# A two-layer MLP in a spectral kernel: the first layer's 512-column products become pairs of 256, and its operands change their byte places

## The chip, the core and the metric

The kernel runs on one core of a Trainium2 chip. Its engines are TensorE (PE, with the weight loads shown as PEld), VectorE (DVE), ScalarE (ACT), GpSimd (POOL) and SyncE (SP), which issues most of the DMAs. The metric is the time of one execution on the device in microseconds. Three runs of the kernel before gave 1358.87, 1359.84 and 1359.89 us, a median of 1359.84.

## The reference

Everything is float32, for 4 sequences of 3136 tokens with 256 features.

```
X = rfft(x, axis=1);  y = irfft(X * (filt_r + 1j*filt_i), n=3136)      # a filter along the sequence
mixed = real(fft(fft(y, axis=1), axis=2));  u = y + mixed               # a Fourier mix
un = layer_norm(u);            v = u + relu(un @ w_ch1) @ w_ch2         # first MLP  (256 -> 1024 -> 256)
vn = layer_norm(v) * g_ln;     out = v + relu(vn @ w_ch1') @ w_ch2'     # second MLP (256 -> 1024 -> 256)
```

## The kernel before

The Fourier transforms of length 3136 = 64 x 49 are written as small matrix products. They run partly ahead of the two MLPs (sequence 0, about the first 100 us) and partly between their products (sequences 1 to 3). The MLPs take the largest part of the time, and the change touches only their first layer.

The tokens are cut into 25 units: units 0 to 23 have 512 tokens (four tiles of 128), unit 24 has 256. A block is one unit in one of the two MLPs, and it has eight steps, one for each 128 of the 1024 hidden features. `steps` lists 400 steps, 384 of them with 512 tokens. In the main loop step i issues the first layer of step i + 2 (`w1_step`, L906), then whatever small work is due at that place (transforms, normalization, the input of later units), then the second layer of step i (`w2_step`, L934), then the evictions of the first layer of step i + 2 (`w1_evict`, L916 on ScalarE and L917 on VectorE). This order is written out by hand; each engine runs its own instructions in it.

To come near float32 accuracy each operand is split in a high and a low part in the type fp32r, and a product a*b becomes high*high + low*high + high*low. So the first layer has six products for a step (two halves of the 256 features, three terms), all of them accumulated in one PSUM bank of 512 columns. The stationary operand (`lhsT`) is a 128 x 128 piece of the weights `w1a` or `w1b`, the moving one (`rhs`) the transposed input `xth` or `xtl` with one column per token. The second layer is the other way round: stationary is a 128 x 128 piece of the first layer's output (`hh` or `hl`, one piece for each tile of 128 tokens), moving a 128 x 256 piece of the weights `w2a` or `w2b`. A step has twelve such products, and they write the four halves of two banks in turn. Every matmul instruction becomes a weight load (LDWEIGHTS) and a product (MATMUL) on the chip.

The other products that stand between the MLP steps are L731 (256 columns, the Fourier mix), L267 (quarter products of 64 x 64 or less for the transforms), and the transposes L618 and L831 (128 columns).

Where a tile lies in SBUF is set by the order of the pools and by `PAD`, seven gaps in 4-byte words, of which `gap2` stands ahead of the first-layer weights, `gap3` ahead of the second-layer weights, `gap5` ahead of the transposed inputs and `gap6` ahead of the h buffers. In bytes modulo 256 the kernel before has its operands at these places:

| operand | tiles | place |
|---|---|---|
| first layer, stationary | w1a, w1b | 32 |
| first layer, moving | xth, xtl | 96 |
| second layer, stationary | hh, hl | 0 |
| second layer, moving | w2a, w2b | 192 |
| L731, stationary | zsh, zsl | 64 |
| L731, moving | chi, clo | 0 |

All slices that these products take begin at multiples of 512 bytes from the tile's start, so each product has its tile's place.

Of the kernel before, what the change touches and what calls it, by code (L numbers as in the profile page):

```python
# [34 lines left out]
CS, o = {}, 0  # L35
# [123 lines left out]
    return c.astype(np.float32)  # L159


PAD = (24, 16, 56, 40, 16, 8, 40)
NA, LAG = 3, 3
AHEAD = 3
DURING = {4: 'a', 8: 'a', 12: 'a', 16: 'a', 18: 'k', 20: 'a', 24: 'ac', 26: 'a', 28: 's', 30: 'f', 31: 'c', 33: 'f', 34: 'c', 35: 'f', 37: 'f', 38: 'c'}
# [18 lines left out]
def spectral_mlp_kernel(ctx: ExitStack, tc, x, ff, ff0, cst, w1a, w2a, gln, w1b, w2b, out):  # L184
    nc = tc.nc
# [3 lines left out]
    def pool(name, bufs, **kw):  # L189
        return ctx.enter_context(tc.tile_pool(name=name, bufs=bufs, **kw))  # L190

    def gap(name, words):
        pool(name, 1).tile([128, words], F32, name=name)

    sm = pool("sm", 4)
    head = pool("head", 1)
    gap("gap0", PAD[0])
    keep = pool("keep", 1)
    gap("gap1", PAD[1])
    keep64 = pool("keep64", 1)  # L200
    uop = pool("uop", 1)
    gap("gap2", PAD[2])
    wp1 = pool("wp1", 1)
    gap("gap3", PAD[3])
    wp2 = pool("wp2", 1)
    wps = {"1": wp1, "2": wp2}
    dram = pool("dram", B, space=DRAM)
    ztp = pool("ztp", 2)
    gap("gap4", PAD[4])
    zsp = pool("zsp", 1)  # L210
# [10 lines left out]
    xdp = pool("xdp", 2, space=DRAM)  # L221
    gap("gap5", PAD[5])
    xtp = pool("xtp", 2)
# [4 lines left out]
    def bank(k=1):  # L228
        t = banks.tile([128, 512], F32, tag="b", name="ps")
        return t if k == 1 else t.rearrange("p (a d) -> p a d", a=k)  # L230
# [9 lines left out]
    def weight(n):  # L240
        if n not in wt:
            wt[n] = wps[n[0]].tile([128, 2, 2, H] if n[0] == "1" else [128, 2, 8, D], F32R, tag="w" + n, name="w" + n)
        return wt[n]
# [417 lines left out]
    def tiles(U):  # L661
        return 4 if U < NU else 2
# [233 lines left out]
    def w1_step(U, layer, m):  # L896
        n = tiles(U) * 128
        assert all(("1" + "ab"[layer], j) in conv_done for j in range(4)), (U, layer, m)
        w = weight("1" + "ab"[layer])
        xt = xt_of[U, layer]  # L900
        ps = bank()
        i = 0
        o = ps[:, :n]
        for k in range(2):
            for a, s in ((0, "h"), (1, "h"), (0, "l")):
                nc.tensor.matmul(out=o, lhsT=w[:, a, k, m * 128:m * 128 + 128], rhs=xt[s][:, k, :n],  # L906
                                 start=i == 0, stop=i == 5)
                i += 1
        w1_out[U, layer, m] = ps

    def w1_evict(U, layer, m):
# [40 lines left out]
    with tc.manual_schedule():  # L952
# [60 lines left out]
        k = 0  # L1013
# [37 lines left out]
        for U in range(NU + 1):  # L1051
            s = index[U, 0]
# [22 lines left out]
        start = 2  # L1075
        for b in range(1, B):
# [22 lines left out]
            n = len(slots)  # L1099
# [4 lines left out]
            start = end + 1  # L1104
# [5 lines left out]
        for s in steps[:2]:  # L1110
            w1_step(*s)
            w1_evict(*s)
        for i, (U, layer, m) in enumerate(steps):
            if i + 2 < len(steps):
                w1_step(*steps[i + 2])
            for f in at.pop(i, []):
                f()
            if i in conv_at:
                run(cw, 1)
            w2_step(U, layer, m)  # L1120
            if i + 2 < len(steps):
                w1_evict(*steps[i + 2])
            if i in conv_at:
                run(cw, 1)
# [86 lines left out]
```

## Time and profile before

| | |
|---|---|
| median of three runs | 1359.84 us |
| the profiled execution | 1360.16 us |
| its span (first to last instruction) | 1358.4 us |
| TensorE busy | 1331.0 us (98%), 8917 products |
| weight loads busy | 1114.0 us (82%), 8917 loads |
| VectorE, ScalarE, GpSimd busy | 797.2, 616.3, 269.7 us |
| mean granted TensorE clock | 0.990 of full speed |

Times count from the start of the span. A row of the timeline gives the start of a piece, its length, its engine and line, what it writes and reads, and how many instructions it merges. The length of a product includes its way through the array, so products that follow each other overlap in the profile; how far apart they really run is read from the starts of the pieces.

### The profile page before, as it was taken

To read this page: it belongs to the slowest core of one execution; us is meant where nothing else is said; L and a number is where in the kernel's file an instruction comes from. 1 tells how busy PE (TensorE), PEld (TensorE's weight loads), DVE (VectorE), ACT (ScalarE), POOL (GpSimd) and SP (SyncE) were. 2 spreads that over 40 slices of the span, in tenths; PEclk is the share of its full clock that TensorE was granted. 3 is DMA by queue.
4 is the path that set the end of the run, shared out by engine and by line. 5 is a ranking of instruction groups with operands and counts; after the bars stand their busy time and mean duration, and the time that the engine had idled before them with its cause. 6 is when DMAs were issued, how large, how long until landed. Compare 5 with 4: busy or idle time off the path is not lost.

```text
span 1358.4 us, 23128 instructions
## 1 busy us (share of the span) xinstructions
PE 1331.0 (98%) x8917; PEld 1114.0 (82%) x8917; DVE 797.2 (59%) x1643; ACT 616.3 (45%) x1205; POOL 269.7 (20%) x277
## 2 busy tenths in 40 slices
PE   8969999999999999999999999999999999999998
PEld 6527887888878888888978888888888988898898
DVE  6967865765445565755554665655545555565353
ACT  5656543454435454544434444545434443444222
POOL 1762022332140322212031221312000000000000
PEclk9969999999999999999999999999999999999999
DMA  8754323442444634613353534524121312332200
GB/s 317 265 183 133 110 78 99 129 134 79 117 144 131 157 96 112 166 48 94 96 161 108 160 103 118 149 77 109 55 63 47 94 41 69 78 85 41 63 17 24
DMA packets 214902, 147.68 MB, mean 109 GB/s; under 512 B 163516, under 2 KB 187196, under 8 KB 214792
## 3 DMA queue, kind: packets, MB, share of 16 engines
q1 hardware_dynamic: 198056, 117.36, 32.1%
q10 hardware_dynamic: 16736, 28.84, 5.9%
q8 instruction: 70, 1.15, 0.4%
q14 instruction: 40, 0.33, 0.1%
HBM read 87.71 MB, written 58.46 MB: 108 GB/s over the span
## 4 chain that ended last, share of the span: by engine, by line
PE 89%; DVE 5%; DMA 2%; issue 1%; ACT 1%; POOL 1%; SPq 1%; ACTq 0%; POOLq 0%; DVEq 0%
PE ps L934 38%; PE ps L906 37%; PE ps L267 7%; PE ps L731 2%; PE ps L320 2%; DMA xr<-in_x 1%; PE ps L365 1%; PE ps L426 1%; PE ps L618 1%; DVE xtl L825 1%; PE ps L831 1%; DVE hl L917 1%; SPq L815 1%; PE ps L382 0%; DVE bs L775 0%
## 5 line engine op out<-in xcount | busy, mean ns | idle before, releaser
L917 DVE SCALAR_TENSOR_TENSOR hl<-ps,hh 128x512 fp32r<-128x512 f32 (+1 forms) x400 | 269.9, 676 | 336.5 <-ACT hh L916 332.0
L916 ACT ACTIVATE hh<-ps 128x512 fp32r<-128x512 f32 (+1 forms) x400 | 232.9, 584 | 368.0 <-PE ps L934 331.7
L906 PE MATMUL ps<-xth,w1a 128*128 128x512 f32 (+1 forms) x800 | 246.3, 390 | 0.0
L906 PE MATMUL ps<-xth,w1b 128*128 128x512 f32 (+1 forms) x800 | 245.4, 388 | 0.0
L934 PEld LDWEIGHTS ps<-w2a,hh 128*128 128x128 f32 x1568 | 203.9, 188 | 36.9 <-issue 24.5
L934 PEld LDWEIGHTS ps<-w2b,hh 128*128 128x128 f32 x1568 | 204.9, 188 | 27.4 <-issue 14.1
L934 PE MATMUL ps<-w2a,hh 128*128 128x256 f32 x1568 | 219.9, 282 | 0.0
L934 PE MATMUL ps<-w2b,hh 128*128 128x256 f32 x1568 | 216.0, 280 | 0.4 <-ACT hh L916 0.2
L779 POOL TENSOR_TENSOR rs<-rs,mhalf 128x4 f32<-128x4 f32 (+1 forms) x51 | 50.8, 996 | 597.4 <-DVE rs L778 511.2
L906 PE MATMUL ps<-xtl,w1a 128*128 128x512 f32 (+1 forms) x400 | 156.0, 390 | 0.3 <-DVE xtl L825 0.3
L906 PE MATMUL ps<-xtl,w1b 128*128 128x512 f32 (+1 forms) x400 | 155.5, 389 | 0.0
L906 PEld LDWEIGHTS ps<-xth,w1a 128*128 128x128 f32 x800 | 136.6, 189 | 18.2 <-issue 1.6
L906 PEld LDWEIGHTS ps<-xth,w1b 128*128 128x128 f32 x800 | 135.7, 188 | 16.3
L790 ACT ACTIVATE xn<-u,nb,rs 128x256 f32<-128x256 f32 x152 | 120.3, 840 | 48.4 <-DVE nb L783 48.1
L934 PE MATMUL ps<-w2a,hl 128*128 128x256 f32 x784 | 123.4, 279 | 1.1 <-DVE hl L917 1.1
L934 PE MATMUL ps<-w2b,hl 128*128 128x256 f32 x784 | 123.3, 278 | 1.1 <-DVE hl L917 0.9
L934 PEld LDWEIGHTS ps<-w2b,hl 128*128 128x128 f32 x784 | 104.1, 188 | 1.9 <-DVE hl L917 1.9
L934 PEld LDWEIGHTS ps<-w2a,hl 128*128 128x128 f32 x784 | 104.5, 189 | 1.3 <-DVE hl L917 1.3
L906 PEld LDWEIGHTS ps<-xtl,w1a 128*128 128x128 f32 x400 | 75.3, 188 | 18.6 <-DVE xtl L825 1.4
L938 DVE TENSOR_TENSOR u<-ps,u 128x512 f32<-128x512 f32 x98 | 63.1, 685 | 46.6 <-PE ps L934 46.6
L906 PEld LDWEIGHTS ps<-xtl,w1b 128*128 128x128 f32 x400 | 75.1, 188 | 17.7 <-DVE xtl L834 0.4
L775 DVE BATCH_NORM_STATS2 bs<-u 128x6 f32<-128x256 f32 x196 | 68.6, 412 | 0.0
(146 smaller groups left out, 1449.3 us busy)
## 6 DMA issues: line engine op xcount, KB each, us to landing
xd<-xn SPq DMA_DIRECT2D x38, 512.0 KB
xtl<-xd SPq DMA_DIRECT2D x152, 128.0 KB
fc<-in_ff SPq DMA_DIRECT2D x34, 512.0 KB
vr<-vd SPq DMA_DIRECT2D x48, 256.0 KB
out<-u SPq DMA_DIRECT2D x24, 512.0 KB
vd<-vst ACTq DMA_DIRECT2D x21, 512.0 KB
xr<-in_x SPq DMA_DIRECT2D x18, 512.0 KB
gd<-gst ACTq DMA_DIRECT2D x36, 256.0 KB
```

The source lines that it names most:

```text
L267: nc.tensor.matmul(out=o[c:c + 64], lhsT=lhs[r:r + k], rhs=rhs[r:r + k], **{"start": True, "stop": True, **kw})
L320: nc.tensor.matmul(out=o, lhsT=cf[at // 512][:k, at % 512:at % 512 + w], rhs=rhs[:k, c0:c1], start=start, stop=stop)
L365: nc.tensor.matmul(out=ps[:, o:o + 128], lhsT=x[:, j, a * 128:a * 128 + 128], rhs=cf[0][:, :128], start=True, stop=True)
L731: nc.tensor.matmul(out=ps[a][:, eo], lhsT=lhs, rhs=cs[eo][r], start=eo == 1 and i == 0, stop=False, skip_group_check=True)
L775: nc.vector.bn_stats(out=st[:, t], in_=u[:, t])
L779: nc.gpsimd.tensor_tensor(out=rs[:, tl], in0=rs[:, tl], in1=mhalf[:, tl], op=ALU.pow)
L790: nc.scalar.activation(out=xs[t], in_=u[:, t].rearrange("p (k a j) -> p j k a", k=2, j=4), func=ACTF.Identity, scale=rs[:, t:t + 1], bias= ...
L906: nc.tensor.matmul(out=o, lhsT=w[:, a, k, m * 128:m * 128 + 128], rhs=xt[s][:, k, :n], start=i == 0, stop=i == 5)
L916: nc.scalar.activation(out=h[:, :n], in_=ps[:, :n], func=ACTF.Relu)
L917: nc.vector.scalar_tensor_tensor(out=l[:, :n], in0=ps[:, :n], scalar=0.0, in1=f32(h[:, :n]), op0=ALU.max, op1=ALU.subtract)
L934: nc.tensor.matmul(out=o[:, t % 2], lhsT=a[:, t * 128:t * 128 + 128], rhs=w[:, b, m], start=m == 0 and i == 0 and t % 2 == 0, stop=m == 7 ...
L938: nc.vector.tensor_tensor(out=u[:, t - 1:t + 1], in0=o, in1=u[:, t - 1:t + 1], op=ALU.add)
```

## The change

`PAD` changes from (24, 16, 56, 40, 16, 8, 40) to (24, 16, 48, 48, 16, 32, 16). The first-layer weights move by -32 bytes, to place 0, and the transposed inputs by +96 bytes, to place 192. The gaps behind them take the difference up, so that all other tiles stay where they are.

`w1_step` issues each product of 512 columns as two of 256, one behind the other with the same weights, into the two halves of the same bank. `start` and `stop` mark the first and the last of the twelve. With 256 tokens (unit 24) there is one product as before. Line numbers behind the function fall by three, so L906 becomes L904 and L934 becomes L931.

```diff
-PAD = (24, 16, 56, 40, 16, 8, 40)
+PAD = (24, 16, 48, 48, 16, 32, 16)
...
-        i = 0
-        o = ps[:, :n]
-        for k in range(2):
-            for a, s in ((0, "h"), (1, "h"), (0, "l")):
-                nc.tensor.matmul(out=o, lhsT=w[:, a, k, m * 128:m * 128 + 128], rhs=xt[s][:, k, :n],
-                                 start=i == 0, stop=i == 5)
-                i += 1
+        terms = [(k, a, s, c) for k in range(2) for a, s in ((0, "h"), (1, "h"), (0, "l")) for c in range(0, n, 256)]
+        for i, (k, a, s, c) in enumerate(terms):
+            nc.tensor.matmul(out=ps[:, c:c + 256], lhsT=w[:, a, k, m * 128:m * 128 + 128], rhs=xt[s][:, k, c:c + 256],
+                             start=i == 0, stop=i == len(terms) - 1, skip_group_check=True)
```

TensorE's order before, in the steady stretch of the program (one step's second layer, the next first layer, the second layer after it; ps is a PSUM bank):

```order
800 L934 MATMUL ps<-w2a,hh 128x256 x8
801 L934 MATMUL ps<-w2a,hl 128x256 x4
802 L906 MATMUL ps<-xth,w1a 128x512 x2
803 L906 MATMUL ps<-xtl,w1a 128x512
804 L906 MATMUL ps<-xth,w1a 128x512 x2
805 L906 MATMUL ps<-xtl,w1a 128x512
806 L934 MATMUL ps<-w2a,hh 128x256 x8
807 L934 MATMUL ps<-w2a,hl 128x256 x4
```

The same place of TensorE's order in the changed kernel:

```order
800 L931 MATMUL ps<-w2a,hh 128x256 x8
801 L931 MATMUL ps<-w2a,hl 128x256 x4
802 L904 MATMUL ps<-xth,w1a 128x256 x4
803 L904 MATMUL ps<-xtl,w1a 128x256 x2
804 L904 MATMUL ps<-xth,w1a 128x256 x4
805 L904 MATMUL ps<-xtl,w1a 128x256 x2
806 L931 MATMUL ps<-w2a,hh 128x256 x8
807 L931 MATMUL ps<-w2a,hl 128x256 x4
```

The order of the groups is the same. Where two and one products of 512 columns stood, four and two of 256 stand, so a step now has 24 products of one width. The other engines and the DMA queues keep their instructions and their order. Signals and waits change in number, not in kind: TensorE's own waits for banks stand on products ten or more places back.

## Rows read from the trace of the kernel before

**Rows 1.** The page: TensorE's busy time; the chain by engine and by line.
```profile
PE 1331.0 (98%) x8917; PEld 1114.0 (82%) x8917; DVE 797.2 (59%) x1643; ACT 616.3 (45%) x1205; POOL 269.7 (20%) x277
...
PE 89%; DVE 5%; DMA 2%; issue 1%; ACT 1%; POOL 1%; SPq 1%; ACTq 0%; POOLq 0%; DVEq 0%
PE ps L934 38%; PE ps L906 37%; PE ps L267 7%; PE ps L731 2%; PE ps L320 2%; DMA xr<-in_x 1%; PE ps L365 1%; PE ps L426 1%; PE ps L618 1%; DVE xtl L825 1%; PE ps L831 1%; DVE hl L917 1%; SPq L815 1%; PE ps L382 0%; DVE bs L775 0%
```

**Rows 2.** The page's groups: the two evictions (busy us, mean ns, idle before).
```profile
L917 DVE SCALAR_TENSOR_TENSOR hl<-ps,hh 128x512 fp32r<-128x512 f32 (+1 forms) x400 | 269.9, 676 | 336.5 <-ACT hh L916 332.0
L916 ACT ACTIVATE hh<-ps 128x512 fp32r<-128x512 f32 (+1 forms) x400 | 232.9, 584 | 368.0 <-PE ps L934 331.7
```

**Rows 3.** Timeline, TensorE, steady steps of unit 23: start us, length us, work.
```profile
1324.87 1.07 PE L934 MATMUL ps<-w2b,hh 128*128 128x256 f32 x8
...
1328.98 0.63 PE L906 MATMUL ps<-xth,w1b 128*128 128x512 f32 x2
...
1330.36 1.07 PE L934 MATMUL ps<-w2b,hh 128*128 128x256 f32 x8
...
1331.72 0.63 PE L906 MATMUL ps<-xth,w1b 128*128 128x512 f32 x2
...
1333.11 1.07 PE L934 MATMUL ps<-w2b,hh 128*128 128x256 f32 x8
```

**Rows 4.** Timeline, TensorE, unit 24 (256 tokens) to the end.
```profile
1351.72 0.40 PE L906 MATMUL ps<-xth,w1b 128*128 128x256 f32 x2
...
1352.43 0.64 PE L934 MATMUL ps<-w2b,hh 128*128 128x256 f32 x4
...
1353.13 0.62 PE L934 MATMUL ps<-w2b,hh 128*128 128x256 f32 x4
...
1353.81 0.62 PE L934 MATMUL ps<-w2b,hh 128*128 128x256 f32 x4
```

**Rows 5.** Timeline, TensorE, first and last of twelve products of L731.
```profile
1090.10 0.28 PE L731 MATMUL ps<-chi,zsh 128*128 128x256 f32 x1
...
1091.39 0.28 PE L731 MATMUL ps<-clo,zmid 128*128 128x256 f32 x1
```

**Rows 6.** Timeline, TensorE, transposes of L618 and the second layer behind them.
```profile
560.66 0.60 PE L618 MATMUL ps<-con,z 128*128 128x128 f32 x4
...
561.22 0.99 PE L934 MATMUL ps<-w2b,hh 128*128 128x256 f32 x7
562.04 0.64 PE L934 MATMUL ps<-w2b,hl 128*128 128x256 f32 x4
562.52 0.62 PE L906 MATMUL ps<-xth,w1a 128*128 128x512 f32 x2
```

**Rows 7.** Timeline, TensorE, end of a second-layer group that follows L267.
```profile
1093.66 0.62 PE L934 MATMUL ps<-w2a,hl 128*128 128x256 f32 x4
1094.12 0.63 PE L906 MATMUL ps<-xth,w1a 128*128 128x512 f32 x2
```

**Rows 8.** Products by form: the 512-column products of L906.
```profile
L906 PE MATMUL ps<-xth,w1a 128*128 128x512 f32 x768 | 240.3, 394 | 0.0
L906 PE MATMUL ps<-xth,w1b 128*128 128x512 f32 x768 | 239.4, 393 | 0.0
...
L906 PE MATMUL ps<-xtl,w1a 128*128 128x512 f32 x384 | 151.5, 395 | 0.3 <-DVE xtl L825 0.3
L906 PE MATMUL ps<-xtl,w1b 128*128 128x512 f32 x384 | 151.1, 393 | 0.0
```

**Rows 9.** The transposes by line: count, ns min/median/max, first and last start.
```profile
L618 PE MATMUL ps<-con,z x102: 272/272/273, 217.9 to 960.0; 128*128 128x128 f32 x102
...
L831 PE MATMUL ps<-con,xn x88: 270/272/476, 95.4 to 1339.0; 128*128 128x128 f32 x88
```

**Rows 10.** The page's DMA queues: packets, MB, share of 16 engines.
```profile
q8 instruction: 70, 1.15, 0.4%
```

## The prediction

> **What bounds the kernel now.** I read the page's busy times and the chain that ended last first. TensorE is busy 98% of the span and 89% of the chain lies on it; the two lines of the MLP, L906 (first layer) and L934 (second layer), hold 37% and 38% of the chain [rows 1]. So a nanosecond off each of their products reaches the end, as long as nobody else becomes late. The waits put to other engines inside the MLP are small: the two evictions that stand between the layers take 0.58 and 0.68 us on ScalarE and VectorE [rows 2], while TensorE needs 2.75 us for one step of both layers, and a product of L906 is issued two steps ahead of the L934 that uses it. About 1.5 us of slack per step is left on VectorE, so its work stays hidden when TensorE's step shrinks by 1%.
>
> Next I read starts, not durations, since the duration of a matmul includes its way through the array (280 ns for a 256-column product that lets the next one start after 113). The start of a piece in the timeline minus the start of the one before it, over the count, is the true pitch.
>
> In the steady stretch, three steps (each 12 products of L934, 6 of L906) take 1333.11 - 1324.87 = 8.24 us, 2.747 us each [rows 3]. Of one step the six 512-column products of L906 take 1333.11 - 1331.72 = 1.39 and 1330.36 - 1328.98 = 1.38 us: 231 ns each, or 115 per 256 columns. The twelve of L934 take 1331.72 - 1330.36 = 1.36 us: 113.3 each.
>
> So the two layers already cost nearly the same per column, and the question is at which pitch a 256-column product of L906 will run. The trace has three places that bear on it.
>
> First, the end of the program, where only L934 runs: 1353.81 - 1353.13 = 0.68 us for six, 113.3 each, with no 512-column product between them [rows 4]. The operands of this line lie at byte 0 (stationary) and 192 (moving) modulo 256.
>
> Second, the last unit has only 256 tokens, so L906 itself runs with 256 columns there, at its old places (32 and 96): 1352.43 - 1351.72 = 0.71 us for six, 118.3 each [rows 4]. L731 (places 64 and 0) does eleven in 1091.39 - 1090.10 = 1.29 us, 117.3 each [rows 5]. So a 256-column product has two pitches in this trace, 113 and 118, and the one layer that reaches 113 is the one whose places the change copies.
>
> Third, L934 itself runs at the slower pitch right after the transposes of L618: from its second product at 561.22 to the start of L906 at 562.52 it needs 1.30 us for 11, 118 each, at the same addresses [rows 6]. A group after the quarter products of L267 is back at 0.46 us for its last four, where the one after the transposes takes 0.48 [rows 6, 7]. So 118 ns is also a rhythm that a stream of products can fall into: it lasts through the twelve, and where I followed it in the timeline the long products of L906 were what came before every clean run of 113.
>
> **The change part by part.** The places: `PAD` moves the four first-layer weight tiles by -32 bytes and the transposed inputs by +96; the sum up to the second layer's weights and up to the h buffers is kept, so nothing else moves. The stationary operand of L906 goes from 32 to 0, its moving one from 96 to 192, as in the second layer. No instruction is added for it.
>
> The split: 2304 products of 512 columns (768 + 384 per weight tile, twice [rows 8]) become 4608 of 256; the 96 of the last unit stay as they are. Each half loads its weights again, 2304 more weight loads. A load takes 188 ns but starts with the product before it, and L934 already runs one load per product at 113 ns, so the loads are hidden under that pitch and not added to it. ScalarE, VectorE, GpSimd and the DMA queues keep their instructions; the evictions still read the whole bank after the last half.
>
> Step with L906 at L934's pitch: 24 x 113.3 = 2.720 us against 2.747 now, 0.027 less. This is the first layer's gain (1.385 - 1.360 = 0.025) and the changeover from L934 to weights at another place. 384 steps have it (2304 / 6): -10.3 us. The starts are given to 0.01 us, over three steps that is 3 ns a step, or 1.3 us on the sum.
>
> The last unit: 96 products of 256 columns, 118.3 to 113.3: -0.5 us.
>
> What is lost: the long products no longer bring the stream back. After transposes the 118 ns rhythm may now last longer. The 102 products of L618, from 217.9 to 960.0 us, make 26 groups and the 88 of L831 22, of which I count ten that leave L934 at 118 [rows 9]: 36 groups. If the rhythm lasts through the L934 group (as now) and the L906 group behind it, that is 36 x 12 x 4.7 ns = +2.0 us. That is the value I take, since L934 leaves the 118 ns within some six products in the two other situations of this trace: after L267 [rows 7], and after the 118 ns products of the last unit, where its first six take 1353.13 - 1352.43 = 0.70 us and the next six 0.68 [rows 4]. The bound below is nothing, the bound above is that it lasts until the next other product: I counted the products of both layers between such groups and the next product of another line, 3426 in 256-column units, 95 a group. Less the 12 that run so already, 36 x 83 x 4.7 = +14.0 us more.
>
> More program: TensorE's stream grows by 4608 instructions. The instruction queue moved 70 packets over the span with 0.4% of the engines' time [rows 10], and no gap inside the two layers is put down to it, so I cost it at nothing; L934 shows that a load and a product every 113 ns are fed.
>
> More waits of TensorE on itself (banks that come free) appear in the order, all on products at least ten back. They are long done, and I cost them at nothing; if each held the stream for one product it would be seen as gaps at bank changes.
>
> Sum: -10.3 - 0.5 + 2.0 = -8.8 us. The profiled execution took 1360.16 us (1.8 around its span); so 1351.4. The median of the runs is 0.3 below the profiled one: 1351.
>
> **The rivals.** (a) The 118 ns rhythm lasts. All as forecast, but a stream that the transposes left in it stays in it until another kind of product comes. For it: at the same addresses the twelve behind L618 stay at 118 to the last, and after the change L906 is to the array what L934 is. Against it: only twelve in a row can be seen now, and the two other entries fall back to 113 within six. -8.8 + 14.0 = +5.2: 1365. It decides against a gain from about 60% of the stretch on.
>
> (b) The place does nothing, and the 113 belongs to how the second layer runs (four products in a row with one moving operand, two banks in turn). Then L906 keeps its 118.3: 4608 x 118.3 - 2304 x 230.8 = +13.4 us; and L934 behind it needs 0.70 us for its first six, as in the last unit, 20 ns more than at 113.3, 384 times: +7.7. Together 1381. For it: every 256-column product of L906 and L731 in this trace has 118, and both add several products to one place in PSUM. Against it: the halves of a bank will be written in turn, as L934 does it, so that half of the explanation would give 113 to the changed L906 too; and L934's way of running does not fix its pitch, as the twelve behind L618 show.
>
> TensorE: Matmul & The Clock Gate of the Trainium skill, in its section "Step-by-step: what each phase is for", says that the weight load has its own read port and takes nothing from the running product. By that rule (b) would hold. The trace shows 113 and 118 for one shape, and at one address pair both, which the rule alone does not give; so (b) stays the lesser rival.
>
> (c) A second load of the same weights is cheaper than one of new weights, and the second half starts earlier: the four transposes of L618 take 0.60 us, the last of them 0.272 by its duration, so they start (0.60 - 0.272) / 3 = 109 ns apart [rows 6, 9]; with 128 columns it is the load that sets this. With 109 for the second halves: 2304 x 4.3 = -9.9 more, 1341.
>
> (d) The gain is made and given back in waits of L906 on its transposed input, which has little slack in the first units. In the rows there is no idle time of a size for it; it would end near 1358.
>
> **How the numbers follow.** Forecast 0.48, (a) 0.21, (b) 0.19, (c) 0.05, (d) 0.07. A measurement of this kernel tells 0.2%, 2.7 us, from no change. Faster: the forecast, with its own range of 1346 to 1357, and (c): 0.53. Same: (d), and 0.10 of (a), where the rhythm lasts for most of the stretch but not all of it: 0.17. Slower: (b) and the rest of (a): 0.30. The range reaches from 1345 to 1369: it holds the forecast, (a) and (d) and leaves out (b) and (c).
>
> **What the changed profile would show.** If right: a step of 2.72 us in the steady stretch; twelve L904 products in 1.36 us; after a group of L618 the L931 and one L904 group at 118, and 113 from the next step. (a): steps of 2.82 us from each L618 group to the next L267. (b): twelve L904 in 1.42 us everywhere, and L931 groups that begin at 117. (c): starts that alternate between 113 and 109. Wrong altogether: gaps on TensorE in the two lines, put to VectorE's hl or to the instruction queue.

## The result, and the profile after

The changed kernel takes 1346.19 us (median of four runs, 1345.02 to 1346.94) against 1359.87 for the kernel before on the same chip: ratio 0.9899, 95% interval 0.9887 to 0.9911, 13.7 us faster. Four more runs on another chip gave 1346.36 and the ratio 0.9902 (0.9887 to 0.9917). The profiled execution took 1346.94 us with a span of 1345.2; before it was 1360.16 and 1358.4, so 13.2 us are to be found between the two profiles. The forecast was 1351; its terms add up to -8.8 us.

TensorE still sets the time. The page of the changed kernel, busy times, chain, and the instruction queue, against [rows 1, 10]:

```profile
PE 1317.5 (98%) x11221; PEld 1211.0 (90%) x11221; DVE 796.5 (59%) x1643; ACT 616.9 (46%) x1205; POOL 270.5 (20%) x277
...
q8 instruction: 88, 1.44, 0.5%
...
PE 92%; DVE 4%; DMA 1%; ACT 1%; issue 1%; POOL 1%; SPq 0%; ACTq 0%; DVEq 0%; POOLq 0%
```

There are 2304 more products and as many more loads, and VectorE, ScalarE and GpSimd do the same work in nearly the same time. What is saved is time between the starts in the two layers. The timeline of TensorE in the steady steps of unit 23 (start us, length us, work), which answers to [rows 3]:

```profile
1312.23 1.07 PE L931 MATMUL ps<-w2b,hh 128*128 128x256 f32 x8
...
1316.31 0.62 PE L904 MATMUL ps<-xth,w1b 128*128 128x256 f32 x4
...
1317.67 1.07 PE L931 MATMUL ps<-w2b,hh 128*128 128x256 f32 x8
1319.03 0.62 PE L904 MATMUL ps<-xth,w1b 128*128 128x256 f32 x4
...
1320.39 0.84 PE L931 MATMUL ps<-w2b,hh 128*128 128x256 f32 x6
```

Three steps take 1320.39 - 1312.23 = 8.16 us, 2.720 each, against 2.747. The twelve products of the first layer need 1317.67 - 1316.31 = 1.36 us, as many of the second layer 1319.03 - 1317.67 = 1.36: 113.3 ns in both layers.

Unit 24, against [rows 4]:

```profile
1338.55 0.39 PE L904 MATMUL ps<-xth,w1b 128*128 128x256 f32 x2
...
1339.23 0.62 PE L931 MATMUL ps<-w2b,hh 128*128 128x256 f32 x4
...
1339.91 0.62 PE L931 MATMUL ps<-w2b,hh 128*128 128x256 f32 x4
```

Six products of L904 take 0.68 us where L906 took 0.71, with the same instructions at other places. The six of L931 behind them take 0.68 where L934 took 0.70. (That the places alone decide this is not so: the run with the new places and 512-column products, below, has the same last unit at 118.)

After the transposes of L618, against [rows 6] (two windows of one timeline):

```profile
556.95 0.60 PE L618 MATMUL ps<-con,z 128*128 128x128 f32 x4
...
557.51 0.96 PE L931 MATMUL ps<-w2b,hh 128*128 128x256 f32 x7
558.31 0.62 PE L931 MATMUL ps<-w2b,hl 128*128 128x256 f32 x4
558.77 0.62 PE L904 MATMUL ps<-xth,w1a 128*128 128x256 f32 x4
```

From the second product to L904 it is 1.26 us for eleven, against 1.30. The last four take 0.46, against 0.48. The 118 ns rhythm that stood behind the transposes before is gone here.

It is not gone from the program. Behind L267 it comes in some places, and then it lasts into the first layer:

```profile
758.40 1.21 PE L931 MATMUL ps<-w2b,hh 128*128 128x256 f32 x8
...
767.26 1.10 PE L931 MATMUL ps<-w2b,hh 128*128 128x256 f32 x8
...
770.09 1.10 PE L931 MATMUL ps<-w2a,hh 128*128 128x256 f32 x8
...
773.00 1.09 PE L267 MATMUL ps<-gr,con 50*64 50x512 f32 x8
```

A step takes 770.09 - 767.26 = 2.83 us here, 118 ns a product, and five steps in a row run at this pitch until the next L267. Counted by single starts, 339 of the 9408 products of the two layers stand in seven such stretches (ten or more products in a row, each 116 to 123 ns before the next), 237 in the second profile of the same kernel. At 4.4 ns each, 339 cost 1.5 us.

### The profile page after: what moved, and what is told of

Read it like the earlier page. It is cut to its first block, busy times and chain, and to the rows that moved or that the text cites. A ratio compares the mean times of both kernels' runs of the same rounds, so it can differ in the third digit from the quotient of the medians.

```text
span 1345.2 us, 27766 instructions
## 1 busy us (share of the span) xinstructions
PE 1317.5 (98%) x11221; PEld 1211.0 (90%) x11221; DVE 796.5 (59%) x1643; ACT 616.9 (46%) x1205; POOL 270.5 (20%) x277
## 3 DMA queue, kind: packets, MB, share of 16 engines
q8 instruction: 88, 1.44, 0.5%
## 4 chain that ended last, share of the span: by engine, by line
PE 92%; DVE 4%; DMA 1%; ACT 1%; issue 1%; POOL 1%; SPq 0%; ACTq 0%; DVEq 0%; POOLq 0%
PE ps L931 39%; PE ps L904 38%; PE ps L267 7%; PE ps L731 2%; PE ps L320 2%; PE ps L365 1%; PE ps L426 1%; PE ps L618 1%; PE ps L831 1%; PE ps L382 0%; DVE hl L914 0%; DMA vd<-vst 0%; DVE bs L775 0%; DMA gd<-gst 0%; DVE wm L873 0%
## 5 line engine op out<-in xcount | busy, mean ns | idle before, releaser
L904 PE MATMUL ps<-xth,w1a 128*128 128x256 f32 x1568 | 243.0, 276 | 0.0
L904 PE MATMUL ps<-xth,w1b 128*128 128x256 f32 x1568 | 242.5, 276 | 0.0
L931 PE MATMUL ps<-w2a,hh 128*128 128x256 f32 x1568 | 219.5, 282 | 0.0
L931 PEld LDWEIGHTS ps<-w2a,hh 128*128 128x128 f32 x1568 | 194.4, 189 | 27.0 <-issue 24.6
L931 PE MATMUL ps<-w2b,hh 128*128 128x256 f32 x1568 | 215.1, 279 | 0.5 <-ACT hh L913 0.5
L904 PEld LDWEIGHTS ps<-xth,w1a 128*128 128x128 f32 x1568 | 207.9, 188 | 1.3 <-issue 1.3
L904 PEld LDWEIGHTS ps<-xth,w1b 128*128 128x128 f32 x1568 | 207.5, 188 | 0.0
L931 PEld LDWEIGHTS ps<-w2b,hh 128*128 128x128 f32 x1568 | 193.2, 188 | 15.4 <-issue 13.8
L904 PE MATMUL ps<-xtl,w1a 128*128 128x256 f32 x784 | 154.6, 277 | 0.0
L904 PE MATMUL ps<-xtl,w1b 128*128 128x256 f32 x784 | 154.3, 276 | 0.0
L931 PE MATMUL ps<-w2b,hl 128*128 128x256 f32 x784 | 122.0, 277 | 1.3 <-DVE hl L914 1.3
L931 PE MATMUL ps<-w2a,hl 128*128 128x256 f32 x784 | 121.9, 277 | 1.1 <-DVE hl L914 1.1
L904 PEld LDWEIGHTS ps<-xtl,w1a 128*128 128x128 f32 x784 | 118.7, 188 | 0.6 <-DVE xtl L825 0.6
L904 PEld LDWEIGHTS ps<-xtl,w1b 128*128 128x128 f32 x784 | 118.7, 188 | 0.2 <-DVE xtl L834 0.2
L931 PEld LDWEIGHTS ps<-w2b,hl 128*128 128x128 f32 x784 | 103.8, 188 | 2.1 <-DVE hl L914 2.1
L931 PEld LDWEIGHTS ps<-w2a,hl 128*128 128x128 f32 x784 | 104.2, 188 | 1.3 <-DVE hl L914 1.3
L935 DVE TENSOR_TENSOR u<-ps,u 128x512 f32<-128x512 f32 x98 | 63.1, 685 | 44.4 <-PE ps L931 44.4
```

The source lines that it names most:

```text
L904: nc.tensor.matmul(out=ps[:, c:c + 256], lhsT=w[:, a, k, m * 128:m * 128 + 128], rhs=xt[s][:, k, c:c + 256], start=i == 0, stop=i == len(t ...
L931: nc.tensor.matmul(out=o[:, t % 2], lhsT=a[:, t * 128:t * 128 + 128], rhs=w[:, b, m], start=m == 0 and i == 0 and t % 2 == 0, stop=m == 7 ...
L935: nc.vector.tensor_tensor(out=u[:, t - 1:t + 1], in0=o, in1=u[:, t - 1:t + 1], op=ALU.add)
```

## The experiments

Theory P says that the pitch of a 256-column product (the time from its start to the next one's) depends on the places of its two operands modulo 256 bytes. Rival S says that the split does it alone, with two halves of a bank written in turn. The forecast's own rival (a) says that a 118 ns rhythm can last.

**The split alone.** `PAD` as before, `w1_step` as in the changed kernel. A further run of the same kernel gave its profile.

```diff
-PAD = (24, 16, 48, 48, 16, 32, 16)
+PAD = (24, 16, 56, 40, 16, 8, 40)
```

> Only the split, PAD as before (first layer at places 32 and 96). Theory P (the places of the two operands modulo 256 bytes set the pitch of a 256-column product): L904 runs at 118 ns as in the last unit of the kernel before, and L931 begins each group at 117: 1372 to 1383 us. Rival S (the split itself, two halves of a bank written in turn, gives 113): 1346, as the changed kernel.

> The split at the old places once more, for its profile. Theory P: twelve L904 products 117 to 118 ns apart (1.41 us a group), the first L931 products behind them at 117 to 120, and a time of about 1373 us as in its timed runs.

Measured: 1373.33 us (the middle one of three runs), ratio 1.0094 (1.0077 to 1.0110); the further run 1370.89. Its timeline of TensorE in a steady step:

```profile
1100.84 0.63 PE L904 MATMUL ps<-xth,w1a 128*128 128x256 f32 x4
...
1102.26 1.09 PE L931 MATMUL ps<-w2a,hh 128*128 128x256 f32 x8
...
1103.64 0.63 PE L904 MATMUL ps<-xth,w1b 128*128 128x256 f32 x4
```

Twelve of L904 take 1.42 us, 118.3 each, and L931 behind them 1.38. S falls: the split without the places is slower than before. It was 1371 to 1373 and not the 1381 of the prediction's (b): summed over the program, the starts of the first layer take 10.4 us more than before where (b) had 13.4, those of the second 3.2 more where it had 7.7. Only the second-layer groups that stand right behind L904 pay the 20 ns; one behind L618 did not:

```profile
562.89 0.60 PE L618 MATMUL ps<-con,z 128*128 128x128 f32 x4
...
564.25 0.62 PE L931 MATMUL ps<-w2b,hl 128*128 128x256 f32 x4
564.71 0.63 PE L904 MATMUL ps<-xth,w1a 128*128 128x256 f32 x4
```

Its last four take 0.46 us, the 113 ns rhythm, at places that were not moved. Nor were those of L731 moved, 64 and 0, and behind L904 it runs at 113 here:

```profile
1097.45 0.28 PE L731 MATMUL ps<-clo,zmid 128*128 128x256 f32 x1
...
1098.13 0.28 PE L731 MATMUL ps<-clo,zmid 128*128 128x256 f32 x1
```

Six starts take 0.68 us, 113.3 each. Before the change eleven took 1.29 us, 117.3 each [rows 5]. By single starts all 24 such groups of L731 run at 113 from about the fourth product on in this run, and at the same places all 24 run at 118 in the changed kernel. So a pair of places does not have one pitch; what ran ahead of the line counts too.

**The places alone.** The new `PAD` with the old `w1_step`.

> Only the places, products of 512 columns as before. Theory P in its strong form (a place costs a product only while the next weights load, 6.6 ns at places 0 and 192): a 512-column product at 213.3 + 6.6 = 220 ns, 11 less than before, 2304 times: 1335 us. P in its weak form (a long product costs twice a short one): 226 to 231, 1347 to 1358. Rival S: 231 as before, 1358 to 1360.

Measured: 1362.23 us, ratio 1.0011 (1.0002 to 1.0021): no gain, rather 0.1% of loss. I had expected one in both forms of P. Its timeline:

```profile
1101.74 0.62 PE L906 MATMUL ps<-xth,w1b 128*128 128x512 f32 x2
...
1103.14 1.07 PE L934 MATMUL ps<-w2a,hh 128*128 128x256 f32 x8
...
1104.50 0.62 PE L906 MATMUL ps<-xth,w1b 128*128 128x512 f32 x2
```

Six products of 512 columns take 1.40 us, 233 each, where they took 1.38 to 1.39 at 32 and 96. So the places at which 256 columns run at 113 bring nothing for 512. Neither half of the change gains anything; together they give 13.7 us.

The last unit of this run has 256 columns at places 0 and 192, the same instructions and places as in the changed kernel, and yet:

```profile
1354.51 0.40 PE L906 MATMUL ps<-xth,w1b 128*128 128x256 f32 x2
...
1355.22 0.63 PE L934 MATMUL ps<-w2b,hh 128*128 128x256 f32 x4
1355.69 0.40 PE L934 MATMUL ps<-w2b,hl 128*128 128x256 f32 x2
1355.92 0.64 PE L934 MATMUL ps<-w2b,hh 128*128 128x256 f32 x4
```

Six of L906 take 0.71 us and six of L934 0.70, 118 and 117 each. By single starts the last 130 products of the program, all at 0 and 192, run at 118. At this pair, too, a product can have either pitch.

**Another order of the twelve.** All six products of the first half of the bank, then the six of the second.

```diff
-        terms = [(k, a, s, c) for k in range(2) for a, s in ((0, "h"), (1, "h"), (0, "l")) for c in range(0, n, 256)]
+        terms = [(k, a, s, c) for c in range(0, n, 256) for k in range(2) for a, s in ((0, "h"), (1, "h"), (0, "l"))]
```

> The changed kernel with the twelve products in another order: all six of the first 256 columns, then all six of the second, so that no weights are loaded twice in a row and six products add to one place of PSUM. Theory P: 113 ns still, 1345 to 1348 us. Rival (the 118 of the last unit and of L731 comes from adding to one place of PSUM several times in a row, or the second load of the same weights is cheaper): 118 ns in L904, 1368 to 1383.

Measured: 1348.85 us, ratio 0.9919 (0.9904 to 0.9934). Its timeline, and its waits of TensorE (us in total, times, longest):

```profile
1101.94 0.39 PE L904 MATMUL ps<-xth,w1b 128*128 128x256 f32 x2
...
1103.31 1.07 PE L931 MATMUL ps<-w2b,hh 128*128 128x256 f32 x8
```

```profile
PE ps L904 <- DVE xtl L825: 1.8, 3, 0.6
```

Twelve take 1.37 us: the pitch of 113 to 114 needs neither the same weights twice nor two halves in turn. The intervals of the two kernels' ratios overlap, so the 2.7 us between them are not certain; 1.8 of them would be this wait, which the changed kernel's list does not have (half by half the last quarter of the input is due at the sixth product and not at the eleventh; that this is the cause is argued). Stretches at 118 hold 470 products here, 131 more than in the changed kernel, which is 0.6 us.

**Absolute places or their difference.** Both operands of the first layer 64 bytes on, to 64 and 0.

```diff
-PAD = (24, 16, 48, 48, 16, 32, 16)
+PAD = (24, 16, 64, 32, 16, 48, 64)
```

> The changed kernel with both operands of the first layer 64 bytes on: stationary at 64, moving at 0, the places of L731. Theory P with absolute places: 117 to 118 ns as L731, 1370 to 1383 us. P with the difference alone (0 to 192 and 64 to 0 are both -64 modulo 256): 113 ns, 1345 to 1348; then L731's 118 comes from something else.

Measured: 1370.94 us, ratio 1.0081 (1.0065 to 1.0096). Its timeline:

```profile
161.41 0.61 PE L904 MATMUL ps<-xth,w1b 128*128 128x256 f32 x4
...
162.76 1.11 PE L931 MATMUL ps<-w2a,hh 128*128 128x256 f32 x8
...
1104.55 0.63 PE L904 MATMUL ps<-xth,w1b 128*128 128x256 f32 x4
...
1105.96 0.29 PE L931 MATMUL ps<-w2a,hh 128*128 128x256 f32 x1
```

1.41 us for twelve at 1104, 118 each, as in L731 at the same places [rows 5]. The difference alone does not do it. But the absolute places do not fix the pitch either: the twelve at 161.41 take 1.35 us, 113 each, at the same 64 and 0, as do those at 179.91; these two of 381 groups come behind a wait of L931 for hl (1.05 and 0.55 us).

**Four pairs in one program.** The weights and the two parts of the input get pools of their own with gaps between, so that each can be placed by itself, and `PAD` gets nine entries. Three runs of the same kind follow below.

```diff
-    wp1 = pool("wp1", 1)
+    wp1b = pool("wp1b", 1)
+    gap("gap7", PAD[7])
+    wp1a = pool("wp1a", 1)
...
-    xtp = pool("xtp", 2)
+    xtps = {"h": pool("xtph", 2)}
+    gap("gap8", PAD[8])
+    xtps["l"] = pool("xtpl", 2)
```

> The changed kernel with four pairs of places in one program: weights of the first MLP at 0, of the second at 32; high part of the input at 192, low part at 96. If both operands must be right (pair theory): 113 ns for w1a with xth alone, 117 to 118 for the three other pairs, 1360 to 1368 us. If the moving place alone decides: 113 for both weights with xth, 1350 to 1355. If the stationary place alone decides: 113 for w1a with both inputs, 1356 to 1361.

Measured: 1371.25 us, ratio 1.0085 (1.0068 to 1.0102). The lines are L908 and L935 here. Its timeline:

```profile
1101.36 0.62 PE L908 MATMUL ps<-xth,w1a 128*128 128x256 f32 x4
1101.81 0.40 PE L908 MATMUL ps<-xtl,w1a 128*128 128x256 f32 x2
1102.04 0.63 PE L908 MATMUL ps<-xth,w1a 128*128 128x256 f32 x4
1102.52 0.40 PE L908 MATMUL ps<-xtl,w1a 128*128 128x256 f32 x2
1102.75 1.09 PE L935 MATMUL ps<-w2a,hh 128*128 128x256 f32 x8
...
1104.13 0.65 PE L908 MATMUL ps<-xth,w1b 128*128 128x256 f32 x4
...
1105.57 1.08 PE L935 MATMUL ps<-w2a,hh 128*128 128x256 f32 x8
```

The first four products, with weights at 0 and input at 192, take 0.45 us, 113 each. From the first one at 96 the other eight of the group take 0.94, 117.5 each. With weights at 32 the twelve take 1.44, 120 each, at either input. So the 113 needs both operands at their places. But four of those eight are at 0 and 192 again, from 1102.04, and take 0.48 us, 120 each: the pair theory gave them 113, and they have it only before another pair has run. The time is above my bound for this reason, and since the pairs with 32 cost 120 and not 118.

**Other pairs.** The same edit with weights at 0 and 128 or 64 and 192, inputs at 64 and 128; then weights at 0 and 128, inputs 32 bytes to either side of 192.

> The changed kernel with the weights of the first MLP at 0, of the second at 128; high part of the input at 64, low part at 128. If the places count modulo 128 only, the pair 128 and 64 is the pair 0 and 192, and w1b with xth runs at 113, the others at 117 to 118. If they count modulo 256: all four at 117 to 118, about 1371 us, unless one of these pairs is another good one.

> The changed kernel with the weights of the first MLP at 64, of the second at 192; high part of the input at 64, low part at 128. Pair theory: none of the four is the pair 0 and 192, all at 117 to 118 and about 1371 us, unless one of them is another good pair; a pitch under 113 in any would point to a faster kernel.

> The changed kernel with the weights of the first MLP at 0, of the second at 128; high part of the input at 224, low part at 160, 32 bytes to either side of the good place. Pair theory: all four pairs at 117 to 121 ns, about 1370 us. If only the 64-byte row counts: (0, 224) is in the row of 192 and stays at 113.

Measured, one run each: 1369.05, 1376.34 and 1371.18 us. A group of L908 in the timelines of the second and of the third:

```profile
1080.07 0.64 PE L908 MATMUL ps<-xth,w1b 128*128 128x256 f32 x4
...
1081.50 1.07 PE L935 MATMUL ps<-w2b,hh 128*128 128x256 f32 x8
```

```profile
1082.60 0.63 PE L908 MATMUL ps<-xth,w1a 128*128 128x256 f32 x4
...
1084.01 1.08 PE L935 MATMUL ps<-w2b,hh 128*128 128x256 f32 x8
```

1.43 and 1.41 us for twelve. Of the sixteen pairs tried in all beside 0 and 192 none let the first layer run steadily at 113, neither the one with both operands 128 bytes on nor those 32 bytes beside it. No group ran under 113. This does not make 0 and 192 the one good pair: in most of these runs two pairs share a group, and in all of them the second layer stays at 0 and 192, so that the first layer's pair differs from that of the line ahead of it. Both layers together at another pair were not tried.

**The second layer taken off its place.** The h buffers 32 bytes on.

```diff
-PAD = (24, 16, 48, 48, 16, 32, 16)
+PAD = (24, 16, 48, 48, 16, 32, 24)
```

> The changed kernel with the h buffers 32 bytes on, so that the second layer's stationary operand lies at 32 and its moving one at 192; the first layer stays at 0 and 192. Pair theory: L904 stays at 113, L931 goes to 117 to 121 ns: 4704 products by 4 to 8 ns, 1365 to 1384 us. Rival (the second layer has its 113 from four products in a row with one moving operand): L931 stays at 113, 1346 us.

Measured: 1375.81 us. Its timeline:

```profile
1082.28 0.62 PE L904 MATMUL ps<-xth,w1a 128*128 128x256 f32 x4
...
1083.65 1.12 PE L931 MATMUL ps<-w2b,hh 128*128 128x256 f32 x8
...
1085.10 0.62 PE L904 MATMUL ps<-xth,w1a 128*128 128x256 f32 x4
```

The twelve of L931 go to 1.45 us, 121 each; the twelve of L904 take 1.37, 114 each. So the second layer's 113 is a matter of place as well, and not only of how it runs.

**L731 at 0 and 192 too, meant as a better kernel (the mix kernel).** The operands of the Fourier mix get the places 0 and 192. The tiles of the transforms behind zsh move by 192 bytes with it, and the tiles between chi and the first layer's weights by -64. The transposed inputs and the h buffers move by 256 bytes, so they keep their places modulo 256.

```diff
-PAD = (24, 16, 48, 48, 16, 32, 16)
+PAD = (8, 16, 64, 48, 64, 48, 16)
```

> The changed kernel with the operands of L731 at the same pair of places (zsh, zsl, zmid from 64 to 0; chi, clo from 0 to 192; the tiles of the transforms behind them move by 192 bytes too). Pair theory: the 300 products of L731 go from 117.5 to 113.3 ns, 1.3 us off the changed kernel, about 1345 us. Rival (the 117 of L731 comes from its three products into one place of PSUM): no change against the changed kernel.

> The changed kernel again, on the same chip as the others of this call: 1345 to 1347 us under every theory; it is what e8 is compared with.

Measured: 1364.99 us, ratio 1.0032 (1.0019 to 1.0044), against 1346.36 for the changed kernel beside it. It is a clear miss: 18.6 us slower where I expected 1.3 faster. Two steps in its timeline, one in each of two units:

```profile
1060.26 1.10 PE L931 MATMUL ps<-w2b,hh 128*128 128x256 f32 x8
...
1063.09 1.10 PE L931 MATMUL ps<-w2b,hh 128*128 128x256 f32 x8
...
1102.16 1.07 PE L931 MATMUL ps<-w2a,hh 128*128 128x256 f32 x8
...
1104.88 1.07 PE L931 MATMUL ps<-w2b,hh 128*128 128x256 f32 x8
```

The same lines at the same places take 2.83 us a step around 1060 and 2.72 around 1102. Followed by single starts, the unit from 1046 to 1092 us runs its 384 products at 118, the one from 1094 to 1138 at 113 but for the first few, the next one at 118 again. The granted clock is 1.00 in all three, so the clock does not tell them apart. About half of the products in the two layers, 4732 of 9408, are in stretches at 118. The changed kernel beside it has 237; 4495 more times 4.4 ns is 19.8 us, and the starts of the two layers, summed, take 19.5 us more; all other lines take 3.6 less. L731 goes along: behind the first layer 12 of its groups run at 113 and 12 at 118, each as the group ahead of it. So rival (a) is a real mechanism: a stream whose products all have the pair 0 and 192 can run at 113 or at 118, and it can keep one for hundreds of products.

## Why the prediction was right, and where it was not

**The bound.** Right: TensorE stays at 98% of the span, and no wait of a size took the gain.

**The pitch of the first layer, -10.3 us.** Right in mechanism and size: a step went from 2.747 to 2.720, the 0.027 that were forecast. Summed over the program, the starts of the first layer's products fall from 553.0 to 542.7 us (the last unit's 0.45 is in that), those of the second layer right behind it by 1.0. All other lines together take the same 242.9 us as before. That the places of the first layer cause it was argued then from the second layer and from the last unit [rows 4]. The split alone (1373) and the places alone (1362) now show it, and that it takes both: with the split and the old places all 358 groups of L904 that follow a group of L931 at 113 run at 118, with the new places all 378 such groups run at 113.

One reason given for it was wrong. The prediction read the 118 of the last unit and of L731 as the price of their places [rows 4, 5]. But L731 runs at 113 at 64 and 0 with the split alone, and the second half of the last unit runs at 118 at 0 and 192 with the places alone. What fits these runs better is that two lines at one pair pass their pitch on, 113 or 118 (the two layers in the changed kernel, and L731 too in the mix kernel), while from one pair to another it can change. Then the gain comes of the first layer having the second's places, whatever these are. This is argued and not shown. So theory P holds in part: the places matter, and they do not set the pitch alone.

**The last unit, -0.5 us.** Right in size: 113.3 for 118.3, 0.45 us, and 0.25 more in the second layer there. That it stayed at 113 was not sure: with the places alone its second half ran at 118 at the same places.

**The loss after the transposes, +2.0 us.** This term failed, in its sign. The rhythm of 118 did not last into L904 behind L618; it did not come at all there. All 27 groups of the second layer behind L618 (the prediction counted 26) ran at 113 from the sixth product on at the latest, where 26 of them had stayed at 118. Summed by single starts, the groups behind L618 lost 1.1 us and those behind L831 0.1: -1.2 us in the place of +2.0, which is 3.2 of the 4.4 us by which the sum was short of the profile's 13.2. Groups behind L267 became shorter too, 12 ns each, 69 of them, which is 0.8 that the forecast had no term for. The rest is in the first two terms.

**Loads, instructions and self-waits at nothing.** Right: 2304 more loads and 18 more packets of the instruction queue leave no gap in the steady steps, and twelve products stand at even starts across the bank changes.

**The rivals.** (b), the place does nothing: refuted by the split alone and by the h buffers at 32. The Trainium skill's page TensorE: Matmul & The Clock Gate, section "Step-by-step: what each phase is for", has the weight load take no read bandwidth from the running product; here the same two instructions cost 113 in one program and 118 in another where only the places of their operands differ, which that rule alone does not give. Whether reading is what they share is not shown. (c), a cheaper second load: refuted, the starts are even, and half by half costs the same pitch. (d): refuted. (a) occurred in the changed kernel in a small part, 339 products or 1.5 us, behind L267 and L831 and at the start of no group behind L618, which the prediction named. The mix kernel shows that it can take the whole gain, at 18.6 us. The chance of 0.21 was not too high; that it stayed small was luck and not an argument of mine.

**What stays open.** What decides the rhythm at the start of a stretch. Of the 27 groups behind L618, 26 are at 118 in the kernel before, 17 with the places alone, 24 with both operands 64 bytes on and 24 in the mix kernel; in the changed kernel none is, half by half none, and with the split alone three. Neither the width of the products ahead of the transposes nor the first layer's places explain all of these, and in the mix kernel tiles of the transforms moved as well. It was not separated. Open too is whether 0 and 192 is a good pair in itself or good because both layers have it: both layers at another pair would tell. And it is not shown why places matter; a collision of the two reads in SBUF would fit, but no run tests it.

## What to carry to other kernels

On a TensorE-bound stream with one weight load for each product, read the pitch from starts, by line and by shape, and compare it with the operands' places (here modulo 256 bytes) and with those of the line ahead: 4 to 7 ns of 113 hung on them here, up to 2% of the whole. Giving the operands of two lines that take turns the same places is worth a try. A change of shape and a change of places can be worth nothing or a loss each and a gain together, so try them as a pair. Read the pitch again in each stretch after every shift of an address, even of another line's tiles, since the same code at the same places ran at either of two rhythms. And do not take the pitch of one stretch for the price of a pair of places.

## What was not expected of the hardware

A stream of 384 products kept 118 ns, or 113, nearly from its start to its end, in the same lines at the same places modulo 256 and at the same granted clock (which of two buffers each used was not compared). A line whose operands did not move, L731, went from 118 to 113 when the line ahead of it moved or changed its shape. And 512 columns at the places where 256 run at 113 are no better, 233 ns for a product against 231.
